# Weight requests regrouped and more blocks begun early around the first two token tiles of a linear-attention and snake-MLP kernel

## The chip, the cores and the metric

The kernel runs on one core of one Trainium2 chip. The metric is the device time of one execution in microseconds (us). The kernel before has a median of 282.01 us over three runs (281.81, 282.01 and 282.65).

The core has a matrix engine (TensorE, "PE" in the profile, its weight loads "PEld"), VectorE ("DVE"), ScalarE ("ACT"), GpSimd ("POOL") and SyncE ("SP"). SP and GpSimd issue the DMA transfers here. Each engine has its own instruction order, fixed when the kernel is built, and waits for the others through semaphores.

## What is computed

Two functions follow each other. The first is linear attention over 8 batches, 8 heads, 576 positions and a head size of 64; the second is a feed-forward block with a snake activation, from 512 to 2048 features and back:

```python
q_s = softmax(q, axis=-1)            # over the 64 features
k_s = softmax(k, axis=2)             # over the 576 positions
kv = np.einsum('bhsd,bhse->bhde', k_s, v)
attn_out = np.einsum('bhsd,bhde->bhse', q_s, kv)
x = attn_out.transpose(0, 2, 1, 3).reshape(4608, 512)
h = x @ w_in
s = np.sin(alpha * h)
g = h + s * s / (alpha + 1e-09)
out = g @ w_out
```

Inputs and output are float32; the kernel works in bfloat16 with float32 sums.

## The kernel before

**Tiling.** The 4608 tokens are worked on in nine tiles of 512 (`nT`). For a tile, the 2048 features of `h` are 16 blocks of 128 (`nN`). One block of `h` is four matmuls of 128x512 (`mm_h`, L275), one for each chunk of 128 features of `x`; the chunks are taken in the order 0, 2, 1, 3 (`KO`, L261). A call of `mm_h` may do a part of the four, so that a block is begun early and ended later. A block then goes through `sine` (L286: a sine on ScalarE, and a square on ScalarE, GpSimd or VectorE, as a letter A, P or D says) and `combine` (L297: VectorE, which writes the block of `g`). `h_slot` (L431) does these for one block, and `flush` lets the combine run one block behind. In tiles 0 and 1, `h_slot` takes the first 4 and 2 blocks as already begun with two of their chunks.

**PSUM banks.** Every block of `h` needs a bank. `BANKS` (L266) says which pool a block of a tile takes its bank from: a, b and l have two banks each, and k is one larger buffer. For tile 1 the string is "aakbbllaabbllaab": blocks 0 and 1 take the two a banks, block 2 the k buffer, 3 and 4 the b banks, 5 and 6 the l banks, 7 and 8 the a banks again, 9 and 10 the b banks again, and so on. A bank can be written again when the combine of the block that had it before is done.

**The second product.** `g @ w_out` is 4 row groups of 128 tokens by 16 blocks of w_out's rows, 64 matmuls for a tile (`mm_o`, L301). For tile 0 it runs through `o_quad` (L439), which keeps all four sums open in the banks of b, b, l and l and goes by quarters of the 16 row blocks: 0 to 3, 4 to 7, 8 to 11, 12 to 15. A sum that is complete is copied out of PSUM (`evac_o`) by the engine that is named for it. `o_quad` and `o_stream` (L591, the form for the later tiles) are generators: `take(os, n)` emits the next n matmuls at that place of the program, and `take(os)` all that are left. In `o_stream` for tile 1, the first two row groups do blocks 0 to 13 each and then 14 and 15 each.

**Attention in between.** The x of tile 0 comes from batch 0, and most of the x of tile 1 from batch 1. While tile 0's `o_quad` runs, batch 1's q and k are exponentiated on ScalarE (`exp_half`), v is cast to bfloat16 (`cast_v1`, L495) on ScalarE, GpSimd and VectorE, `wide_mm` forms the product of k and v for half of the heads (18 matmuls of 128x130), `wide_norm` scales it on VectorE, and `attn_x` forms x for that half of the heads (4 matmuls on quarters of the array). After `attn_x(1, 0)`, ScalarE copies chunk 0 of x and VectorE chunk 2 into `xT`; after `attn_x(1, 1)`, VectorE copies chunks 1 and 3.

**Loads.** The weights are cast to bfloat16 by the DMA and are requested by GpSimd (`load_win`, L107; `load_wout`, L110). Before tile 0, GpSimd requests w_in in pieces, the last of them being columns 1536 to 2047 (blocks 12 to 15), and then w_out's row blocks 0 to 7. The rest is requested from inside tile 0's loop through the table `late` (L476): at block 6 the first half of batch 1's q, at 8 w_out's row blocks 8 to 11, at 10 row blocks 12 and 13, and at 12 the second half of q and then k and v of batch 1 in five requests (`load_kv1`, L468). q, k and v go through SP's queue, w_in and w_out through GpSimd's. Row blocks 14 and 15 come as float32 through SP's queue after batch 1's v into two spare tiles (L488) and are cast into `wout` later, one by GpSimd and one by ScalarE (L544). After them on SP's queue come the last 64 positions of q for batches 0 and 1 (`q8`) and the three loads of batch 2.

Of the kernel before, what the change touches and what calls it, by code (L numbers as in the profile page):

```python
# [15 lines left out]
F32 = mybir.dt.float32  # L16
# [7 lines left out]
def kernel(  # L24
# [14 lines left out]
    nc = tc.nc  # L39
# [7 lines left out]
    nN = d_ff // 128  # L47
    MF = 512
# [12 lines left out]
    spool = ctx.enter_context(tc.tile_pool(name="spool", bufs=4))  # L61
# [45 lines left out]
    def load_win(c0, c1, cc=slice(0, 4)):  # L107
        nc.gpsimd.dma_start(out=win[:, cc, c0:c1], in_=win_v[:, cc, c0:c1])  # L108

    def load_wout(n0, n1):  # L110
        nc.gpsimd.dma_start(out=wout[:, n0:n1, :], in_=wout_v[:, n0:n1, :])
# [151 lines left out]
    G = {}  # L263

    HP = {}
    BANKS = {0: "aabbkllaabbkllaa", 1: "aakbbllaabbllaab", 2: "aabbopaabbopaabb"}  # L266

    def bank(kind):
# [6 lines left out]
    def mm_h(t, ni, k0=0, k1=4):  # L275

        if ni == 0 and k0 == 0:
            G[t] = gpool.tile([128, nN, MF], BF16, name="g")
        hp = HP[t, ni] if k0 else bank(BANKS.get(t, 3 * "aabb" + "abba")[ni])
        HP[t, ni] = hp  # L280
        for k in range(k0, k1):
            nc.tensor.matmul(hp, win[:, KO[k], ni * 128:(ni + 1) * 128],  # L282
                             xT[:, KO[k], t * MF % NX:t * MF % NX + MF], start=(k == 0), stop=(k == 3))
        return hp
# [75 lines left out]
    load_win(0, 512, slice(1, 4, 2))  # L360
    for c in range(2, 6):
        load_win(256 * c, 256 * c + 256)
    load_win(1536, 2048)
    for c in range(2):
        load_wout(4 * c, 4 * c + 4)

# [62 lines left out]
        mm_h(0, ni, ki, ki + 1)  # L429

    def h_slot(t, ni, sq, lag):  # L431
        hp = mm_h(t, ni, 2 if ni < (4, 2, 0)[min(t, 2)] else 0)
        lag.append((t, ni, hp, sine(t, ni, hp, sq)))

    def flush(lag, keep):
# [15 lines left out]
    def take(it, n=1000):  # L451
        for _ in range(n):
            if next(it, 0) == 0:
                return
# [4 lines left out]
    with ES:  # L459
        def load_q1(ii):  # L460
            if ii == 0:
                staged["q", 1] = stage.tile([128, 4, J, D], F32, name="st_q", tag="st")
            st = staged["q", 1]
            DVE_CP(st[:, ii, 0, 0:1], zero)
            nc.sync.dma_start(out=st[:, ii::2, 0:8].rearrange("p i j d -> p i (j d)"),
                              in_=src_view(q, 1)[:, ii::2, 0:8 * D])

        def load_kv1():  # L468
            for n in "kv":
                staged[n, 1] = stage.tile([128, 4, J, D], F32, name=f"st_{n}", tag="st")  # L470
            for n, t, ii, j0, j1 in (("k", k, 0, 0, J), ("v", v, 0, 0, J), ("k", k, 1, 0, J),
                                     ("v", v, 1, 0, 5), ("v", v, 1, 5, J)):
                nc.sync.dma_start(out=staged[n, 1][:, ii::2, j0:j1].rearrange("p i j d -> p i (j d)"),
                                  in_=src_view(t, 1)[:, ii::2, j0 * D:j1 * D])

        late = {6: lambda: load_q1(0), 8: lambda: load_wout(8, 12), 10: lambda: load_wout(12, 14),  # L476
                12: lambda: (load_q1(1), load_kv1())}
        for ni in range(nN):
            h_slot(0, ni, "DPPAPPAPPAAPPAPD"[ni], lag)
            flush(lag, 1)  # L480
            if ni in late:
                late[ni]()
        flush(lag, 0)

        accs = [bank(kind) for kind in "bbll"]
        os = o_quad(0, accs, [DVE_CP, ACT_CP, DVE_CP, DVE_CP])

        late_w = [spool.tile([128, MF], F32, name="s") for _ in range(2)]  # L488
        for n in range(2):
            nc.sync.dma_start(out=late_w[n], in_=wout_v[:, 14 + n])  # L490
        for b in range(2):
            nc.sync.dma_start(out=q8[:, :, b], in_=src_view(q, b)[:, :, 8 * D:J * D])
        load_batch(2)
# [34 lines left out]
        exp_half("k", 1, 1)  # L528
        take(os, 9)
        transpose_q1(1, DVE_CP)  # L530
        take(os, 1)
        wide_mm(1, 0)
        wide_norm(1, 0)
        take(os, 3)
        cast_v1(1)
        xa = [bank("a") for _ in range(2)]
        attn_x(1, 0, 0, 8, xa)
        for x in range(2):
            (ACT_CP, DVE_CP)[x](xT[:, 2 * x, MF:2 * MF], xa[x])
        take(os, 1)  # L540
        wide_mm(1, 1)
        wide_norm(1, 1)
        for n, eng in ((0, GP_CP), (1, ACT_CP)):
            eng(wout[:, 14 + n], late_w[n])  # L544
        exp_to(A["qe", 1][:, J - 2:J], q8)
        for ni, ki in ((0, 0), (1, 0), (0, 1), (1, 1)):
            mm_h(1, ni, ki, ki + 1)
        xb = ps_k.tile([128, 2, MF], F32, name="kvp", tag="a")
        attn_x(1, 1, 0, 8, [xb[:, x] for x in range(2)])
        DVE_CP(xT[:, 1:4:2, MF:2 * MF], xb)  # L550
        nc.scalar.activation(zero, zero, AX.Sin)
        take(os)
        scale_q8 = norm_q8()
        load("q", q, 3)
        load("k", k, 3)
# [35 lines left out]
    def o_stream(t, eng=DVE_CP):  # L591
        order = [(j, ni) for j in range(4) for ni in range(nN)]
        if t == 1:
            order = [(j, ni) for n0, n1 in ((0, nN - 2), (nN - 2, nN)) for j in range(2) for ni in range(n0, n1)] + order[2 * nN:]
        acc = {}
        for j, ni in order:
            if ni == 0:
                acc[j] = bank("b" if t == 1 and j == 0 else "op"[j % 2])
            mm_o(t, j, ni, acc[j])
            if ni == nN - 1:  # L600
                evac_o(t, j, acc[j], eng)
            yield
# [4 lines left out]
    os = o_stream(1)  # L607
# [131 lines left out]
```

## Time and profile before

| | |
|---|---|
| median of three runs | 282.01 us |
| the profiled execution | 283.14 us |
| its span, first to last instruction | 281.3 us |
| TensorE busy | 268.4 us, 95% of the span |
| ScalarE busy | 224.2 us, 80% |
| VectorE busy | 187.1 us, 67% |
| GpSimd busy | 80.2 us, 28% |
| granted TensorE clock | 0.999 of full speed |

The profile is of one execution. Its span leaves out what lies before the first and after the last instruction. Matmuls are pipelined: a 128x512 matmul is shown with some 379 ns, but the next one starts earlier, so the distance of starts is what tells how fast they run, and a busy TensorE need not be at its peak. A few matmul records are missing, so a group can show three where four were run. A line number can be that of a helper, as for `mm_h` (its matmul is L282) and `mm_o` (L302).

The time by stretches of the program shows where the edits lie (from the span's start; busy time of each engine in us):

| stretch, us | what TensorE does | PE | DVE | ACT | POOL | DMA, GB/s |
|---|---|---|---|---|---|---|
| 0 to 13 | batch 0's attention | 7.28 | 7.97 | 8.96 | 7.68 | 289 |
| 13 to 24.55 | tile 0, blocks to 11 | 10.75 | 7.92 | 10.23 | 8.23 | 187 |
| 24.55 to 35.39 | tile 0's last blocks, w_out rows 0 to 7 | 10.54 | 8.81 | 7.22 | 4.57 | 268 |
| 35.39 to 43.38 | w_out rows 8 on, batch 1's attention | 7.78 | 5.54 | 4.32 | 1.65 | 384 |
| 43.38 to 59.81 | tile 1's blocks | 16.32 | 14.86 | 15.20 | 8.78 | 323 |
| 59.81 to 75.60 | w_out for tile 1, batch 2's attention | 15.58 | 15.16 | 13.74 | 10.92 | 239 |
| 75.60 to 100 | tile 2 | 24.24 | 17.92 | 21.44 | 15.63 | 188 |
| 100 to 281.30 | tiles 3 to 8 | 175.96 | 108.96 | 143.13 | 22.70 | 113 |

### The profile page before, as it was taken

What the parts mean: (1) busy time and instruction counts of PE and PEld (TensorE: products, weight loads), DVE (VectorE), ACT (ScalarE), POOL (GpSimd) and SP (SyncE); (2) the same over time, 40 slices, a digit from 0 to 9 for tenths busy, and PEclk for the clock granted to TensorE, in tenths of its full rate; (3) what the DMA queues carried; (4) which work ended last, traced back from release to release, by engine and by line L of the source; (5) the groups of instructions that cost most, each with busy time, mean ns of one, the idle gap of its engine ahead of it and who ended that gap; (6) DMA issues with size and microseconds to landing.
All of it is one profiled execution on the core that took longest, in us unless ns stands there. A gap on an engine that the chain in (4) does not pass through costs nothing.

```text
span 281.3 us, 4775 instructions
## 1 busy us (share of the span) xinstructions
PE 268.4 (95%) x1814; PEld 124.2 (44%) x1843; DVE 187.1 (67%) x279; ACT 224.2 (80%) x321; POOL 80.2 (28%) x75
## 2 busy tenths in 40 slices
PE   3899999999999999999999999999999999999994
PEld 1434454444444444444444444444444444444443
DVE  2968867999878767766776677577775555555422
ACT  4799457999588999899989998999877777777400
POOL 2959112678667450215011500350000000000000
PEclk9999999999999999999999999999999999999999
DMA  7999999795699039811981199125011111111143
GB/s 258 299 185 224 276 385 401 266 356 198 156 245 379 3 76 294 336 37 43 328 332 37 40 267 384 37 51 123 10 30 37 37 40 37 38 42 44 41 100 75
DMA packets 39607, 46.06 MB, mean 164 GB/s; under 512 B 17040, under 2 KB 22944, under 8 KB 39584
## 3 DMA queue, kind: packets, MB, share of 16 engines
q1 hardware_dynamic: 33952, 41.11, 46.1%
q0 software_dynamic: 5472, 4.52, 9.8%
q8 instruction: 14, 0.23, 0.3%
q10 hardware_dynamic: 160, 0.13, 0.2%
q14 instruction: 9, 0.07, 0.1%
HBM read 36.71 MB, written 9.44 MB: 164 GB/s over the span
## 4 chain that ended last, share of the span: by engine, by line
PE 87%; DMA 8%; POOL 2%; issue 1%; ACT 0%; SPq 0%; DVE 0%
PE hp L282 38%; PE op L302 37%; DMA wout<-in_moe_w_out_dram 4%; PE hp L302 2%; DMA win<-in_moe_w_in_dram 2%; PE lp L282 2%; DMA st_k<-in_k_dram 2%; PE kvp L173 2%; PE lp L302 1%; PE op L282 1%; PE op L709 1%; PE hp L237 1%; POOL s L292 1%; PE xp L237 1%; PE kvp L282 1%
## 5 line engine op out<-in xcount | busy, mean ns | idle before, releaser
L298 DVE SCALAR_TENSOR_TENSOR g<-s,inva_sb,hp 128x512 bf16<-128x512 f32 x129 | 95.1, 745 | 58.9 <-ACT s L290 53.3
L282 PE MATMUL hp<-xT,win 128*128 128x512 bf16 x508 | 128.8, 379 | 0.8 <-DMA win<-in_moe_w_in_dram 0.4
L302 PE MATMUL op<-wout,g 128*128 128x512 bf16 x463 | 117.6, 379 | 1.7 <-issue 1.3
L288 ACT ACTIVATE s<-hp,alpha_sb 128x512 f32<-128x512 f32 x129 | 87.0, 684 | 21.8 <-PE hp L282 20.3
L282 PEld LDWEIGHTS <-win 128*128 128x128 bf16 x576 | 55.6, 98 | 68.4 <-DMA win<-in_moe_w_in_dram 1.8
L302 PEld LDWEIGHTS <-g 128*128 128x128 bf16 x560 | 53.4, 98 | 65.4 <-issue 2.9
L290 ACT ACTIVATE s<-s 128x512 f32<-128x512 f32 x112 | 70.7, 632 | 3.6
L292 POOL TENSOR_TENSOR s<-s 128x512 f32<-128x512 f32 x28 | 29.5, 1066 | 17.8 <-ACT s L288 17.7
L152 POOL TENSOR_TENSOR qn<-qe,qs 128x1152 bf16<-128x1152 bf16 x11 | 23.2, 2128 | 30.7 <-DVE qs L146 26.3
L314 DVE COPY o<-op 128x512 f32<-128x512 f32 (+2 forms) x32 | 21.1, 660 | 9.7 <-PE op L302 7.4
L137 POOL CAST vb<-st_v 128x1152 bf16<-128x1152 f32 x12 | 14.4, 1228 | 44.5 <-DMA st_v<-in_v_dram 44.2
L118 ACT ACTIVATE qe<-st_q 128x1152 bf16<-128x1152 f32 (+2 forms) x18 | 17.7, 1026 | 6.3 <-DMA st_q<-in_q_dram 6.1
L118 ACT ACTIVATE ke<-st_k 128x1152 bf16<-128x1152 f32 x16 | 17.9, 1153 | 2.6 <-DMA st_k<-in_k_dram 2.6
L145 DVE TENSOR_REDUCE qs<-qe 128x36 f32<-128x2304 bf16 x5 | 12.8, 2552 | 8.3 <-ACT qe L118 8.3
L302 PE MATMUL hp<-wout,g 128*128 128x512 bf16 x45 | 12.0, 379 | 0.5 <-DMA wout<-in_moe_w_out_dram 0.3
L118 ACT ACT_TABLE_LOAD x7 | 9.0, 1283 | 0.8 <-PEq L723 0.7
L302 PE MATMUL lp<-wout,g 128*128 128x512 bf16 x32 | 9.2, 379 | 0.1
L369 PE MATMUL warm<-st_q,ident 128*128 128x512 f32 (+1 forms) x6 | 4.1, 806 | 4.7 <-DMA st_q<-in_q_dram 4.7
L282 PE MATMUL lp<-xT,win 128*128 128x512 bf16 x32 | 7.7, 379 | 0.4 <-DMA win<-in_moe_w_in_dram 0.4
L250 DVE CAST xT<-xp 128x1024 bf16<-128x1024 f32 (+1 forms) x7 | 7.4, 1065 | 0.0
L298 DVE SCALAR_TENSOR_TENSOR g<-s,inva_sb,lp 128x512 bf16<-128x512 f32 x8 | 5.7, 739 | 0.4 <-POOL s L292 0.4
L108 POOL DMA_DIRECT2D win<-in_moe_w_in_dram x8 | 5.9, 772 | 0.0
(98 smaller groups left out, 137.2 us busy)
## 6 DMA issues: line engine op xcount, KB each, us to landing
out_dram<-o SPq DMA_DIRECT2D x70, 128.0 KB, 2.3
st_q<-in_q_dram SPq DMA_DIRECT2D x6, 1152.0 KB, 6.3
st_k<-in_k_dram SPq DMA_DIRECT2D x6, 1152.0 KB, 9.1
st_v<-in_v_dram SPq DMA_DIRECT2D x6, 1152.0 KB, 11.3
st_k<-in_k_dram SPq DMA_DIRECT2D x4, 576.0 KB, 8.3
st_q<-in_q_dram SPq DMA_DIRECT2D x4, 512.0 KB, 6.2
wout<-in_moe_w_out_dram POOLq DMA_DIRECT2D x3, 512.0 KB, 13.7
win<-in_moe_w_in_dram POOLq DMA_DIRECT2D x5, 256.0 KB, 7.9
```

The costliest lines, as they stand in the source:

```text
L118: nc.scalar.activation(dst[:, :, ii * 128:(ii + 1) * 128].rearrange("p j (x d) -> p x j d", x=2), src[:, ii::2], AX.Exp)
L137: engs[ii](vv[:, 2 * ii:2 * ii + 2, :, 0:D], staged["v", b][:, ii::2])
L145: nc.vector.tensor_reduce(qs, A["qe", b].rearrange("p j (i d) -> p j i d", i=4), axis=AXL.X, op=ALU.add)
L152: engs[ii % len(engs)].tensor_tensor(qn[:, ii, 0:j1].rearrange("p j (x d) -> p j x d", x=2), qe[:, ii], part.unsqueeze(3).to_broadcast([12 ...
L250: eng(xT[:, c, d0:d0 + m - n], xp[..., n:m])
L282: nc.tensor.matmul(hp, win[:, KO[k], ni * 128:(ni + 1) * 128], xT[:, KO[k], t * MF % NX:t * MF % NX + MF], start=(k == 0), stop=(k == 3))
L288: nc.scalar.activation(s, hp, AX.Sin, scale=alpha_sb[:, ni:ni + 1])
L290: nc.scalar.activation(s, s, AX.Square)
L292: nc.gpsimd.tensor_tensor(s, s, s, op=ALU.mult)
L298: nc.vector.scalar_tensor_tensor(G[t][:, ni], in0=s, scalar=inva_sb[:, ni:ni + 1], in1=hp, op0=ALU.mult, op1=ALU.add)
L302: nc.tensor.matmul(acc, G[t][:, ni, j * 128:(j + 1) * 128], wout[:, ni, :], start=(ni == 0), stop=(ni == nN - 1))
L314: eng(o[:, cols], acc)
```

## The change

Seven edits, all in the first two tiles:

1. The last w_in piece (columns 1536 to 2047) is requested in two parts, chunks 0 and 2 first, then 1 and 3.
2. w_out's row blocks 8 to 11 are requested in two parts, 8 and 9 at block 8 of tile 0's loop and 10 and 11 at block 10.
3. Row blocks 12 to 15 are requested by GpSimd in two parts at block 14. The float32 tiles for 14 and 15, their two requests on SP's queue and the two casts are gone. GpSimd's requests for 12 to 15 now stand behind three more squares in its order, those of blocks 11, 12 and 14.
4. In tile 0, blocks 12 and 13 both do chunks 0 and 2 before block 12 goes on.
5. Around batch 1's attention, more of `o_quad` is taken before each step (6 instead of 1 before the first `wide_mm`, 3 instead of 1 after the first `attn_x`), so that both wide products come later; one matmul is left for the last `take`. The sums are copied out by ScalarE, VectorE, ScalarE, VectorE.
6. In tile 1, blocks 0, 1, 3, 4 and 5 are begun early: 0, 1 and 3 with three of the four chunks, 4 and 5 with two (the table `BEGUN`). Chunks 1 and 3 of x are copied one by one by VectorE.
7. In `o_stream` for tile 1 the first pass ends at block 12 instead of 14.

TensorE runs the same 1840 matmuls; their order changes between the end of tile 0's blocks and tile 1's w_out.

```diff
+    BEGUN = {0: {ni: 2 for ni in (0, 1, 2, 3, 12, 13)}, 1: {0: 3, 1: 3, 3: 3, 4: 2, 5: 2}}
...
-    load_win(1536, 2048)
+    for r in range(2):
+        load_win(1536, 2048, slice(r, 4, 2))
...
-        hp = mm_h(t, ni, 2 if ni < (4, 2, 0)[min(t, 2)] else 0)
+        hp = mm_h(t, ni, BEGUN.get(t, {}).get(ni, 0))
...
-        late = {6: lambda: load_q1(0), 8: lambda: load_wout(8, 12), 10: lambda: load_wout(12, 14),
-                12: lambda: (load_q1(1), load_kv1())}
+        late = {6: lambda: load_q1(0), 8: lambda: load_wout(8, 10), 10: lambda: load_wout(10, 12),
+                12: lambda: (load_q1(1), load_kv1()), 14: lambda: (load_wout(12, 14), load_wout(14, 16))}
         for ni in range(nN):
+            for n in (12, 13) if ni == 12 else ():
+                mm_h(0, n, 0, 2)
...
-        os = o_quad(0, accs, [DVE_CP, ACT_CP, DVE_CP, DVE_CP])
-
-        late_w = [spool.tile([128, MF], F32, name="s") for _ in range(2)]
-        for n in range(2):
-            nc.sync.dma_start(out=late_w[n], in_=wout_v[:, 14 + n])
+        os = o_quad(0, accs, [ACT_CP, DVE_CP, ACT_CP, DVE_CP])
+
...
         transpose_q1(1, DVE_CP)
-        take(os, 1)
+        take(os, 6)
         wide_mm(1, 0)
         wide_norm(1, 0)
         take(os, 3)
-        cast_v1(1)
         xa = [bank("a") for _ in range(2)]
         attn_x(1, 0, 0, 8, xa)
         for x in range(2):
             (ACT_CP, DVE_CP)[x](xT[:, 2 * x, MF:2 * MF], xa[x])
-        take(os, 1)
+        cast_v1(1)
+        take(os, 3)
+        for ni, ki in ((0, 0), (1, 0), (0, 1), (1, 1)):
+            mm_h(1, ni, ki, ki + 1)
         wide_mm(1, 1)
         wide_norm(1, 1)
-        for n, eng in ((0, GP_CP), (1, ACT_CP)):
-            eng(wout[:, 14 + n], late_w[n])
         exp_to(A["qe", 1][:, J - 2:J], q8)
-        for ni, ki in ((0, 0), (1, 0), (0, 1), (1, 1)):
+        take(os)
+        for ni, ki in ((3, 0), (3, 1), (4, 0)):
             mm_h(1, ni, ki, ki + 1)
         xb = ps_k.tile([128, 2, MF], F32, name="kvp", tag="a")
         attn_x(1, 1, 0, 8, [xb[:, x] for x in range(2)])
-        DVE_CP(xT[:, 1:4:2, MF:2 * MF], xb)
+        for x in range(2):
+            DVE_CP(xT[:, 2 * x + 1, MF:2 * MF], xb[:, x])
         nc.scalar.activation(zero, zero, AX.Sin)
-        take(os)
+        for ni, ki in ((4, 1), (5, 0), (5, 1), (0, 2), (1, 2), (3, 2)):
+            mm_h(1, ni, ki, ki + 1)
...
-            order = [(j, ni) for n0, n1 in ((0, nN - 2), (nN - 2, nN)) for j in range(2) for ni in range(n0, n1)] + order[2 * nN:]
+            order = [(j, ni) for n0, n1 in ((0, 12), (12, nN)) for j in range(2) for ni in range(n0, n1)] + order[2 * nN:]
```

## Prediction

> **What bounds the kernel now.** I read the page's busy times and chain first, then TensorE's waits, then the time-ordered rows of each engine from 13 to 75 us, where every edit lies.
>
> ```profile
> PE 268.4 (95%) x1814; PEld 124.2 (44%) x1843; DVE 187.1 (67%) x279; ACT 224.2 (80%) x321; POOL 80.2 (28%) x75
> ...
> PE 87%; DMA 8%; POOL 2%; issue 1%; ACT 0%; SPq 0%; DVE 0%
> ```
>
> TensorE is the bound: the chain that ends last runs through it for 87% of the span, and the DMA share is the places where it stood waiting for a load. The edits keep TensorE's work the same, so they can only move its waits. TensorE's waits from 13 to 80 us, and its rows around two of them (start, duration, operation, count, idle time before and what ended it):
>
> ```profile
> PE lp L282 <- DMA win<-in_moe_w_in_dram: 0.4, 1, 0.4
> PE hp L282 <- DMA win<-in_moe_w_in_dram: 0.4, 1, 0.4
> PE hp L302 <- DMA wout<-in_moe_w_out_dram: 0.3, 1, 0.3
> ...
> 23.36 0.81 PE L282 MATMUL kvp<-xT,win 128*128 128x512 bf16 x3
> 24.55 1.90 PE L282 MATMUL lp<-xT,win 128*128 128x512 bf16 x8 [0.39 <-DMA win<-in_moe_w_in_dram]
> ...
> 34.49 0.59 PE L302 MATMUL lp<-wout,g 128*128 128x512 bf16 x2
> 35.39 0.38 PE L302 MATMUL hp<-wout,g 128*128 128x512 bf16 x1 [0.30 <-DMA wout<-in_moe_w_out_dram]
> ```
>
> Back to back, eight 128x512 matmuls start over 1.73 us (24.55 to 26.29), 0.216 us each; the 379 ns of the groups overlap. So starts give the true stalls. Block 11 (kvp, four matmuls, one record missing) should hand over at 23.36 + 4 x 0.216 = 24.22, and block 12 begins at 24.55: 0.33 us lost to the last w_in piece. The pair at 34.49 should hand over at 34.92, and row block 8 begins at 35.39: 0.47 us lost to w_out. The third wait (15.57) lies before every edit.
>
> **Part 1, two requests for the last w_in piece and for w_out 8 to 11: -0.80 us.** The first half of w_in serves chunks 0 and 2, and now blocks 12 and 13 both do these first: the second half is wanted 4 x 0.216 us after 24.22, at 25.08, and the whole piece was there by 24.55. Rows 8 and 9 are wanted at 34.92 - 0.33 = 34.59. The four rows took 35.35 - 31.07 = 4.3 us of their queue (landings of the last two w_out requests, issue plus time to landing), so half of them land near 33.2. Rows 10 and 11 are wanted 8 x 0.216 later, at 36.3, and land near 35.35. Both stalls go, 0.80 us. GpSimd issues one more request before the first square (0.75 us); it sits idle 2.48 us there. The bounds are -0.80 and, if neither half lands early, 0.
>
> The Trainium skill, "DMA: Bandwidth & Descriptors", Rules for kernel authors, advises at least 1 MiB per transfer for full bandwidth, which speaks against halves. Here the four w_in requests of 256 KB written before the last land 1.28 to 1.34 us apart, and the 512 KB one 3.31 us after them, so halves are not slower in this trace; if they were, 0.33 us of the gain would be in doubt.
>
> **Part 2, w_out 12 to 15 on GpSimd's queue: +0.9 us, with part of it from k.** Rows 12, 13 (256 KB as written) were requested at 25.34 right behind 8 to 11. Now they come after square 14, at about 29.3, and 14, 15 after them at 30.1. They ran on SP's queue behind v before, into a float32 tile, with a cast each on GpSimd (0.61) and ScalarE (0.62), both casts with idle time before them; taking these away gives TensorE nothing. SP's queue loses those two requests, so batch 2's loads (first issued at 39.46) go out sooner, but behind v in the same queue, and cost k and v nothing. Two queues share the DMA engines there, and what each gets is seen in the DMA view for 32 to 33 us and in the stretches (the last two figures are DMA share and GB/s):
>
> ```profile
> q1 hardware_dynamic: 95, 0.19, 56.9%
> q0 software_dynamic: 92, 0.09, 54.1%
> ...
> 35.00:37.00 2.00, 1.64 (x8) 0.78 (x8) 0.92 (x1) 1.05 (x1) 0.00 (x0) 1.00 1.05 397
> 37.00:39.00 2.00, 2.00 (x17) 1.13 (x15) 1.93 (x4) 1.17 (x1) 0.00 (x0) 1.00 1.04 400
> 39.00:41.00 2.00, 2.00 (x27) 1.19 (x26) 0.87 (x2) 0.88 (x2) 0.62 (x1) 1.00 1.08 392
> ```
>
> q0 is GpSimd's queue, q1 is SP's: packet for packet they alternate, and a q0 packet of half the bytes costs the engines as much. From 35 to 41 us the engines are full with k and v of batch 1. Alone, q0 moves 209 GB/s (30 to 31 us), so 256 KB more of it takes 262 KB / 209 GB/s = 1.25 us of all engines, and k and v behind it land up to that much later. Bounds: 0 (all of it after k) and 1.45 (16 packets for each DMA engine at 0.09, half of the 0.18 us between shared ones).
>
> What waits for k is on ScalarE:
>
> ```profile
> 40.85 1.17 ACT L118 ACTIVATE ke<-st_k 128x1152 bf16<-128x1152 f32 x1 [0.70 <-DMA st_k<-in_k_dram]
> 42.56 0.59 ACT L539 CAST xT<-hp 128x512 bf16<-128x512 f32 x1 [0.54 <-PE hp L237]
> ...
> 47.58 0.69 ACT L288 ACTIVATE s<-hp,alpha_sb 128x512 f32<-128x512 f32 x1
> ```
>
> The second half of k is exponentiated the moment it lands, and x's chunk 0 is copied behind it. The change puts a PSUM evacuation (0.57) between them. With k at 40.85 + 1.25 = 42.10: exponential to 43.15 (1.05 where two follow each other), evacuation to 43.65, copy to 44.24, seen by TensorE at 44.28. TensorE wants that chunk for block 0 of tile 1. Before, it got there at 43.38; now 0.80 earlier by part 1, seven w_out matmuls later (63 against 56 done; 1.51), without the second wide product (0.62 and 0.1 for the change of tile shape): 43.38 - 0.80 + 1.51 - 0.72 = 43.37. The wait is 44.28 - 43.37 = 0.91. With k on time the copy ends at 43.03, 0.34 ahead: 0 is the lower bound, and 1.45 gives 1.1.
>
> Rows 14, 15 lie inside this. They are wanted at 40.38 - 0.80 + 5 x 0.216 = 40.66. Rows 12, 13 landed 2.94 us after 8 to 11 while sharing, so the like piece behind lands at 38.29 + 2.9 = 41.2 (stall 0.55); at the lone rate 39.5 (none). A stall there only spends part of the 0.91, because k is waited for in any case. GpSimd's and VectorE's casts of v have more room: the second wide product comes 0.9 us after the chunk.
>
> **Part 3, three matmuls instead of eight ahead of chunk 1: +0.15.** attn_x of the second half starts at T; its copy started 0.46 later (44.35, 44.81), and half of it takes 0.69, ready at T + 1.15. TensorE: 0.34 + 3 x 0.216 = T + 0.99. Bounds 0 and 0.3.
>
> **Part 4, blocks begun early: +0.94.** This is the largest new wait. Blocks 0, 1 and 3 have three of four chunks before the first sine can run, 4 and 5 two. From the start of block 0's last matmul, at t, TensorE has 1 + 1 + 4 + 1 + 2 + 2 + 3 x 4 = 23 matmuls to block 9, which it reaches at t + 4.97; before, 31 (6.7). Block 9 takes the bank of block 3, free when VectorE has combined block 3:
>
> ```profile
> 49.43 1.41 DVE L298 SCALAR_TENSOR_TENSOR g<-s,inva_sb,hp 128x512 bf16<-128x512 f32 x2 [0.77 <-POOL s L292]
> 50.75 1.00 DVE L294 TENSOR_TENSOR s<-s 128x512 f32<-128x512 f32 x1
> 51.68 0.73 DVE L298 SCALAR_TENSOR_TENSOR g<-s,inva_sb,kvp 128x512 bf16<-128x512 f32 x1
> 52.33 1.39 DVE L298 SCALAR_TENSOR_TENSOR g<-s,inva_sb,hp 128x512 bf16<-128x512 f32 x2
> ```
>
> First sine 47.58, GpSimd's square to 49.39, then VectorE without a gap until block 3 is combined at 52.33 + 0.74 = 53.07: 5.49 us that the change doesn't shorten. A sine starts 0.42 after its block's last matmul (76.21 to 76.63 in tile 2). The bank is free at t + 5.91; the wait is 5.91 - 4.97 = 0.94. Bounds: 0.63 if the square at 50.75 takes the 0.69 of the one at 29.60, 1.1 if ScalarE adds a wait.
>
> The Trainium skill, "Advanced Engine Details and Errata", VectorE Performance Modes, says that GpSimd shares VectorE's second SBUF port, so the two block each other. The slow square lies beside GpSimd's 50.17 to 52.66; by that rule it stays 1.00 as long as the two stay neighbours, which they do, so I keep 0.94.
>
> After block 9 ScalarE paces the tile and the delay is passed on; TensorE has no slack later to take it back. The two blocks fewer in o_stream's first pass cost nothing: block 12 is wanted 5.2 us after it starts, and the last combine followed it by 3.3.
>
> **Sum:** -0.80 + 0.91 + 0.15 + 0.94 = +1.20. The profiled span becomes 281.3 + 1.2 = 282.5. The profiled execution took 283.14 with its span of 281.3, and the runs shown have a median of 282.01; I put the same difference on it: 283.2 us.
>
> **Rivals.**
> - *k is not late* (the rows fill gaps or come behind k): -0.80 + 0.15 + 0.94 = +0.3, 282.3. For it: the bounds of part 2. Against: no free DMA time in the stretches.
> - *Faster: TensorE loses only its waits.* If block 3's combine ends 0.9 us sooner after the first sine, because squares and evacuations no longer crowd VectorE (it had 0.77 idle ahead of 49.43), and k is on time, -0.80 remains: 281.2; decides if the wait at block 9 is under 0.1. Against: the chain is GpSimd's square plus five VectorE operations in a row.
> - *The loads slip further:* GpSimd's late requests give rows 12, 13 after 38.49, when they are wanted (landing 38.29, 0.2 to spare), and k a further 1 us: 0.91 + 1.0 in part 2, 284.2. For it: the small margin.
> - *The edits don't act* (the halves land together): part 1 gives 0 and all else stands, 284.0; counted with the last.
>
> **How the numbers follow.** A measurement of this kernel tells 0.3% (0.85 us) from no change: 281.16 to 282.86. Chances: forecast 0.48 (own range 282.7 to 283.6; 0.06 of it under the bound), k on time 0.24, only waits lost 0.14 (0.10 of it past the bound), slipping loads or no action 0.14. Faster 0.10, same 0.34, slower 0.56. The range reaches from the second rival, 281.3, to the third, 284.2.
>
> **What would show it.** Right: no wait at the lp of block 12 nor at row 8; a ScalarE exponential of k starting near 42.1 and TensorE waiting for ScalarE's copy of xT before block 0 of tile 1; a TensorE wait for VectorE of 0.6 to 1.1 us at block 9 of tile 1. Wrong: k's exponential at or before 41.2, or block 9 begun without a wait; then the time is 0.9 lower for each.

## The result: 284.04 us, 0.6% slower

| | before | changed |
|---|---|---|
| median, six runs each | 282.39 us (281.81 to 282.80) | 284.04 us (283.92 to 284.24) |
| first profiled execution | 283.14 us, span 281.3 us | 284.09 us, span 282.3 us |
| second profiled execution | 281.94 us, span 280.1 us | 283.74 us, span 282.0 us |

The changed kernel takes 1.0061 of the time before, 95% interval 1.0047 to 1.0074; a second measurement (below) gives 1.0053, 1.0034 to 1.0072. It is slower, as forecast, and inside the range of 281.3 to 284.2. It is 0.84 us above the forecast of 283.2, though, and above the forecast's own range of 282.7 to 283.6. Part of the 0.84 is the base: the prediction had three runs of the kernel before (282.01), and the median of six is 282.39. As a difference, +1.20 was forecast and +1.65 measured (+1.48 the second time). The forecast's parts were not all right, and the second execution of the kernel before, read below, is what tells them apart.

First the page of the changed kernel, first execution: the busy line, and the chain that ended last by engine.

```profile
PE 272.3 (96%) x1843; PEld 125.3 (44%) x1843; DVE 187.0 (66%) x279; ACT 223.8 (79%) x321; POOL 81.9 (29%) x77
...
PE 82%; DMA 5%; issue 4%; DVE 3%; ACT 3%; POOL 2%; SPq 0%; POOLq 0%; ACTq 0%
```

The 3.9 us more of busy TensorE are no work: this trace has all matmul records (1843 for 1843 weight loads; before, 1814). What is new is in the chain: VectorE and ScalarE now hold 3% of it each (GpSimd had its 2% before, too), and the loads 5% instead of 8%. TensorE's waits from 13 to 80 us show where (line, releaser: us in total, times, longest):

```profile
PE hp L283 <- DVE g L299: 0.9, 1, 0.9
```

The two waits for w_in and the one for w_out that this view showed before are gone, and one wait for a combine has come. Its place is in the time-ordered rows of TensorE (start, duration, operation, count, and in brackets the idle time before and what ended it):

```profile
51.41 1.89 PE L283 MATMUL hp<-xT,win 128*128 128x512 bf16 x8
54.18 1.02 PE L283 MATMUL hp<-xT,win 128*128 128x512 bf16 x4 [0.89 <-DVE g L299]
```

The eight matmuls are blocks 7 and 8 of tile 1; at 0.216 us a start they should hand over at 51.41 + 1.73 = 53.14, and block 9 starts at 54.18: 1.05 us lost (the 0.89 counts from the drawn end of the last matmul). VectorE's rows of the same execution:

```profile
50.49 1.41 DVE L299 SCALAR_TENSOR_TENSOR g<-s,inva_sb,hp 128x512 bf16<-128x512 f32 x2 [1.59 <-POOL s L293]
51.81 1.00 DVE L295 TENSOR_TENSOR s<-s 128x512 f32<-128x512 f32 x1
52.74 0.73 DVE L299 SCALAR_TENSOR_TENSOR g<-s,inva_sb,kvp 128x512 bf16<-128x512 f32 x1
53.39 1.39 DVE L299 SCALAR_TENSOR_TENSOR g<-s,inva_sb,hp 128x512 bf16<-128x512 f32 x2
```

Block 3 is the first of the pair at 53.39 and is done by 54.13; TensorE goes on 0.05 later. It is the same row of five operations behind GpSimd's square as before, 1.06 us later. What ScalarE does ahead of it:

```profile
41.15 1.16 ACT L118 ACTIVATE ke<-st_k 128x1152 bf16<-128x1152 f32 x1 [1.24 <-DMA st_k<-in_k_dram]
...
43.04 0.59 ACT L539 CAST xT<-hp 128x512 bf16<-128x512 f32 x1 [0.23 <-PE hp L237]
...
48.64 1.27 ACT L289 ACTIVATE s<-hp,alpha_sb 128x512 f32<-128x512 f32 x2 [2.23 <-PE hp L283]
```

k's second exponential starts at 41.15, only 0.30 later than in the first profile of before (40.85), and the copy of chunk 0 waits for TensorE rather than TensorE for it. By this comparison k would hardly be late. That comparison misleads, as the first experiment shows.

### The profile page after: what moved, and what is told of

Its sections match the earlier page's. It is cut to its first block, busy times and chain, and to the rows that moved or that the text cites. A ratio compares the mean times of both kernels' runs of the same rounds, so it can differ in the third digit from the quotient of the medians.

```text
span 282.3 us, 4801 instructions
## 1 busy us (share of the span) xinstructions
PE 272.3 (96%) x1843; PEld 125.3 (44%) x1843; DVE 187.0 (66%) x279; ACT 223.8 (79%) x321; POOL 81.9 (29%) x77
## 4 chain that ended last, share of the span: by engine, by line
PE 82%; DMA 5%; issue 4%; DVE 3%; ACT 3%; POOL 2%; SPq 0%; POOLq 0%; ACTq 0%
PE op L303 37%; PE hp L283 35%; DMA st_v<-in_v_dram 3%; ACT s L289 2%; PE warm L371 2%; PE kvp L173 2%; DVE g L299 2%; POOL s L293 1%; DMA st_q<-in_q_dram 1%; PE op L283 1%; PE hp L303 1%; PE op L713 1%; PE hp L237 1%; PE xp L237 1%; PE lp L283 1%
## 5 line engine op out<-in xcount | busy, mean ns | idle before, releaser
L303 PE MATMUL op<-wout,g 128*128 128x512 bf16 x480 | 120.4, 379 | 0.0
L303 PE MATMUL hp<-wout,g 128*128 128x512 bf16 x48 | 12.8, 379 | 0.0
L371 PE MATMUL warm<-st_q,ident 128*128 128x512 f32 (+1 forms) x6 | 4.9, 958 | 4.7 <-DMA st_q<-in_q_dram 4.7
L108 POOL DMA_DIRECT2D win<-in_moe_w_in_dram x9 | 6.6, 783 | 0.0
```

Source lines behind the costliest of these rows:

```text
L303: nc.tensor.matmul(acc, G[t][:, ni, j * 128:(j + 1) * 128], wout[:, ni, :], start=(ni == 0), stop=(ni == nN - 1))
L371: nc.tensor.matmul(warm.rearrange("p a b -> p (a b)")[:, 0:n], ident, staged["q", 0][:, 0, 0:8].rearrange("p j d -> p (j d)")[:, 0:n], sta ...
```

## The experiments

Twelve runs followed, in groups of four, four, two and two, with the kernel before measured again beside each group (medians 282.29, 282.06, 281.93 and 282.08 us over 15 to 21 runs); the ratios are to those. "Lost" is by how much the distance between two matmul starts exceeds the one at the same place in before_again or, where the order is new, the one between such matmuls when nothing is waited for. Where a matmul's record is missing (its weight load is there), its own 0.216 us are taken off. Losses under 0.1 are left out, and so is the start of tile 0, which comes 0.8 us later in fewer_begun, 0.5 in win_split_only and 0.1 in late_rows than in before_again.

| run | median, us | ratio, 95% interval | span of its profile | what TensorE lost between 13 and 62 us |
|---|---|---|---|---|
| before_again | 282.39 | 1.0009 [0.9988, 1.0030] | 280.1 | nothing |
| after_again | 283.77 | 1.0053 [1.0034, 1.0072] | 282.0 | 1.05 block 9; 0.24 w_out row 14; 0.37 copy of chunk 0; 0.21 chunk 1 |
| dma_only | 283.87 | 1.0054 [1.0036, 1.0072] | 281.4 | 0.96 and 0.20 at casts of v |
| begin_only | 285.33 | 1.0102 [1.0074, 1.0131] | 284.2 | 1.05 block 9; 0.21 chunk 1; 0.19 copies of chunks 0 and 2; 1.76 and 0.41 w_out; 0.78 w_in |
| k_at_9 | 285.48 | 1.0111 [1.0093, 1.0128] | 283.1 | 0.39 block 9; 1.69 and 0.27 q's transposes; 0.32 cast of v; 0.38 copy of chunk 0; 0.21 chunk 1 |
| fewer_begun | 284.24 | 1.0061 [1.0041, 1.0080] | 283.1 | none at block 9; 0.87 and 0.38 chunk 1; 0.48 cast of v; 0.40 copy of chunk 0 |
| split_only | 282.47 | 1.0014 [1.0001, 1.0027] | 280.4 | 0.54 at a combine of tile 0 |
| rows_at_10 | 284.78 | 1.0092 [1.0076, 1.0109] | 283.0 | 1.26 at a combine of tile 0; 1.05 block 9; 0.21 chunk 1; 0.19 copies of chunks 0 and 2; 0.14 q's second transposes |
| late_rows | 283.41 | 1.0046 [1.0030, 1.0063] | 281.8 | 1.05 block 9; 0.21 chunk 1; 0.19 copies of chunks 0 and 2 |
| win_split_only | 282.48 | 1.0008 [0.9993, 1.0022] | 281.3 | 0.71 w_out row 8; 0.10 w_in's second half |
| three_three | 281.92 | 0.9996 [0.9986, 1.0007] | 280.0 | nothing |
| before_third | one run, 281.95 | | 280.1 | nothing |

### before_again and after_again: the same two kernels, profiled a second time

> The kernel before, once more, with a profile of its own. Theory 'order' (the waits at w_in's last piece and at w_out row 8 belong to the kernel and come in every execution): stalls of about 0.33 and 0.47 us again, span 281 to 281.6, ratio 1.000. Theory 'chance' (the first profile caught loads that are late only now and then, which would explain why the medians differ by 1.65 us and the two profiles' TensorE rows by 0.83): one of the stalls is missing here and the span is 0.4 to 0.8 us shorter.

> The changed kernel, once more. Theory 'order': a wait of 0.9 to 1.1 us at block 9 of tile 1 again, 0.2 before chunk 1, none at w_in or w_out; ratio 1.005 to 1.007. If the slow first transposes (8.21 to 9.27 us) of its first profile were chance, its tile 0 starts 0.5 us earlier here and the span is near 281.8; if they belong to the kernel, they are there again.

TensorE's waits from 13 to 80 us, kernel before, second execution, all that the view lists:

```profile
PE hp L302 <- issue: 0.2, 1, 0.2
PE op L302 <- issue: 0.2, 1, 0.2
```

No wait for a load is left; the two lines of 0.2 are missing matmul records. The chain on this execution's page says the same in one line, against the 87% and 8% of the first:

```profile
PE 96%; DMA 1%; issue 1%; DVE 0%
```

So the three load waits of the first profile do not come in every execution. Whether row 8 of w_out is waited for goes by when the request for rows 8 to 11 lands. The list of DMA issues from 24 to 45 us (count, size, median us from issue to landing), kernel before, first execution:

```profile
wout<-in_moe_w_out_dram POOLq DMA_DIRECT2D x1, 512.0 KB, 10.8
```

and the second:

```profile
wout<-in_moe_w_out_dram POOLq DMA_DIRECT2D x1, 512.0 KB, 8.9
```

1.9 us between two executions of one program, where the stall was 0.47. The first one had been measured at 283.14 us when the median of its runs was 282.01: it was one of the longer executions, and the 0.80 us of stalls are of the size of that difference.

The same goes for k. ScalarE's rows in the second execution of before:

```profile
39.55 1.16 ACT L118 ACTIVATE ke<-st_k 128x1152 bf16<-128x1152 f32 x1 [0.69 <-DMA st_k<-in_k_dram]
...
46.43 1.27 ACT L288 ACTIVATE s<-hp,alpha_sb 128x512 f32<-128x512 f32 x2
```

and in the second execution of the changed kernel:

```profile
41.27 1.16 ACT L118 ACTIVATE ke<-st_k 128x1152 bf16<-128x1152 f32 x1 [0.92 <-DMA st_k<-in_k_dram]
...
48.31 1.26 ACT L289 ACTIVATE s<-hp,alpha_sb 128x512 f32<-128x512 f32 x2 [1.88 <-PE hp L283]
```

Compared like with like, k's exponential comes 1.72 us later, not 0.30, and the first sine of tile 1 1.88 us later. The waits of the changed kernel in this execution:

```profile
PE hp L283 <- DVE g L299: 0.9, 1, 0.9
PE hp L283 <- ACT xT L539: 0.2, 1, 0.2
```

Now TensorE does wait for ScalarE's copy of chunk 0, as the prediction had it (0.37 by starts), after 0.24 for w_out's row 14, the 57th matmul of the sum, which starts at 40.36 as its load lands, too short a stop for this view. In the first execution of the changed kernel TensorE began tile 0 at 13.57 us instead of 12.68, which gave k 0.9 us more: its lateness was hidden by another one. With 0.21 at chunk 1, the changed kernel loses 1.05 + 0.24 + 0.37 + 0.21 = 1.87 us by these places; its span is 282.0 - 280.1 = 1.9 us longer.

### dma_only: the loads' edits with tile 1 as before

```diff
 against the changed kernel
-        os = o_quad(0, accs, [ACT_CP, DVE_CP, ACT_CP, DVE_CP])
+        os = o_quad(0, accs, [DVE_CP, ACT_CP, DVE_CP, DVE_CP])
...
-        take(os, 6)
+        take(os, 1)
         wide_mm(1, 0)
...
```

The rest of edits 5 to 7 is taken back in the same way; edits 1 to 4 stay.

> Edits 1 to 4 alone: the requests and tile 0's order; batch 1's attention and tile 1 as before. Theory 'order' (the loss is tile 1's order, the gain the requests): no wait at block 9, both stalls gone, TensorE 0.6 to 0.8 us earlier from row 8 on, unless k is late; ratio 0.997. Rival 'requests' (the loss comes from w_out's rows sharing the DMA engines with k and v): k's second exponential starts 0.5 us or more later and TensorE waits for x's chunk 0 of tile 1; ratio 1.002 or more.

TensorE's waits, 13 to 80 us:

```profile
PE kvp L184 <- ACT vb L499: 0.9, 1, 0.9
```

The loads' edits alone cost as much as the whole change. In the old order TensorE reaches the first wide product of batch 1 at 39.3 and loses 0.96 us to ScalarE's cast of v, and 0.20 more before the second. No wait at block 9. The late loads are a loss of 1.2 us in this execution (1.3 by the spans; 1.6 by the medians, the profiled execution being the quickest of nine) when nothing is put in front of them; the changed order of tile 1 puts five more w_out matmuls there, and in after_again the waits for casts of v are gone.

Why k and v are late is seen in one microsecond, 36 to 37 us, in the queues of the kernel before, second execution (packets, MB, share of 16 DMA engines):

```profile
q1 hardware_dynamic: 189, 0.41, 104.6%
```

and of the changed kernel, second execution:

```profile
q1 hardware_dynamic: 98, 0.21, 59.5%
q0 software_dynamic: 102, 0.09, 53.6%
```

SP's queue (q1), which carries k and v, moves half of what it moved, and the two queues alternate packet by packet: 98 to 102. The Trainium skill, "DMA: Bandwidth & Descriptors", section "Queues, rings and completion order", says that each DMA engine goes round between the queues it has work for, a packet at a time; these counts agree. Since a packet of GpSimd's queue carries less here (0.09 MB in 102 against 0.21 in 98), the DMA engines moved 0.30 MB in this microsecond where they had moved 0.41.

### begin_only: the new order of tile 1 with the old loads

```diff
 against the changed kernel
-    for r in range(2):
-        load_win(1536, 2048, slice(r, 4, 2))
+    load_win(1536, 2048)
...
+        late = {6: lambda: load_q1(0), 8: lambda: load_wout(8, 12), 10: lambda: load_wout(12, 16),
+                12: lambda: (load_q1(1), load_kv1())}
...
-            for n in (12, 13) if ni == 12 else ():
-                mm_h(0, n, 0, 2)
```

> Edits 5 to 7 with the requests of before (w_out 8 to 11 in one request; 12 to 15 in one request at block 10, since the new order wants 14 and 15 earlier than the float32 tiles have them). Theory 'order': the wait of about 1 us at block 9 is here too, and the two stalls of before: ratio 1.003 to 1.008. Rival 'requests': no wait at block 9 beyond 0.3 us, ratio 1.000 or less.

TensorE's waits, 13 to 80 us:

```profile
PE hp L303 <- DMA wout<-in_moe_w_out_dram: 1.8, 2, 1.6
PE hp L283 <- DVE g L299: 0.9, 1, 0.9
PE lp L283 <- DMA win<-in_moe_w_in_dram: 0.6, 1, 0.6
```

Four rows in one request came too late for row 12 (1.76 us), a stall that neither kernel has, so its time says little. What it does show: the wait at block 9 is 1.05 again when w_out's rows are requested another way. k is not early here (its second exponential starts at 41.90), so late_rows repeats the question without these rows.

### late_rows: the new order with k and v alone on the DMA engines

```diff
 against the changed kernel
-        nc.tensor.matmul(acc, G[t][:, ni, j * 128:(j + 1) * 128], wout[:, ni, :],
+        nc.tensor.matmul(acc, G[t][:, ni, j * 128:(j + 1) * 128], wout[:, ni - 4 * (t == 0 and ni > 11), :],
...
-                12: lambda: (load_q1(1), load_kv1()), 14: lambda: (load_wout(12, 14), load_wout(14, 16))}
+                12: lambda: (load_q1(1), load_kv1())}
...
         cast_v1(1)
+        load_wout(12, 16)
```

Tile 0's sums leave rows 12 to 15 out and read rows 8 to 11 again, in as many matmuls.

> The changed kernel without the late loads' traffic: rows 12 to 15 of w_out are requested behind the second cast of v, some 12 us later, and tile 0's output reads rows 8 to 11 a second time in their place (that tile's values are so changed; all later tiles read the right rows). k and v then share the window with nothing. Theory 'order': the new order of tile 1 costs its 1.05 at block 9 and 0.2 at chunk 1 whatever the loads do; the excesses of 0.24 at 39.9 and 0.37 at 42.9 vanish, v lands 1.5 us earlier or more, and the median is 1.2 to 1.4 above the kernel before, 283.2 to 283.5, ratio 1.004 to 1.005. Rival 'requests': block 9's wait is only the lateness of k and v handed on; with early loads it falls below 0.4 and the median is within 0.5 of the kernel before. Rival 'GpSimd': the one later request holds GpSimd for some 1 us in front of its cast or square, the wait at chunk 1 or at block 9 grows, and the median is at 283.8 or above.

TensorE's waits, 13 to 80 us, all but two of 0.2 that are missing records:

```profile
PE hp L283 <- DVE g L299: 0.9, 1, 0.9
```

Its rows at the start of tile 1:

```profile
42.39 0.82 PE L303 MATMUL lp<-wout,g 128*128 128x512 bf16 x3
43.14 1.13 PE L283 MATMUL hp<-xT,win 128*128 128x512 bf16 x4
```

The theory "order" holds: the wait for row 14 is gone, block 9's is 1.05 to the hundredth, and the median is 1.48 us above the kernel before (283.41 against 281.93). k's second exponential starts at 38.30, far from mattering, and yet 0.19 is lost at block 0: three matmuls from 42.39 hand over at 43.04 and the next starts at 43.14, when ScalarE's copy of chunk 0 (42.50 to 43.09) is done, and a matmul later TensorE stops 0.10 for VectorE's copy of chunk 2, whose bank block 1 takes. By starts the new order loses 1.05 + 0.21 + 0.19 = 1.45. The 0.19 does not hang on k, and no step of the prediction had it. The order alone (1.48) and the loads alone (1.58, dma_only) each cost about what the whole change costs (1.48, after_again): they do not add up.

### fewer_begun: seven early matmuls instead of thirteen

```diff
 against the changed kernel
-... 1: {0: 3, 1: 3, 3: 3, 4: 2, 5: 2}}
+... 1: {0: 2, 1: 2, 3: 2, 4: 1}}
...
-        for ni, ki in ((4, 1), (5, 0), (5, 1), (0, 2), (1, 2), (3, 2)):
-            mm_h(1, ni, ki, ki + 1)
```

> The changed kernel without the six matmuls of blocks 0, 1, 3, 4 and 5 between the first sine's table load and the block loop: they go back to their blocks, the other seven early ones stay. Theory 'first sine': these six cover the two copies of chunk 1; without them TensorE waits 1.0 to 1.3 us for the copies, the first sine starts at the same time or up to 0.3 earlier, and block 9 is reached after block 3's combine, so the wait of 1.05 there vanishes; what is saved at one place is lost at the other and the median stays within 0.3 of 283.8, ratio 1.004 to 1.006. Rival 'early starts cost': the six push block 0's last matmul and so the first sine back by their own 1.3 us, and without them the sine starts 1 us earlier and the median falls by 0.7 or more, to about 283.0.

TensorE's rows:

```profile
48.28 0.38 PE L283 MATMUL hp<-xT,win 128*128 128x512 bf16 x1 [0.80 <-DVE xT L553]
48.88 0.81 PE L283 MATMUL hp<-xT,win 128*128 128x512 bf16 x3 [0.22 <-DVE xT L553]
...
53.19 3.19 PE L283 MATMUL hp<-xT,win 128*128 128x512 bf16 x14
```

The stall moves from block 9 to the copies of chunk 1, and blocks 7 to 10 run through without one (the view ends at 56 us and shows 14 of their 16 matmuls). At the copies 0.87 + 0.38 = 1.25 us are lost, where after_again loses 0.21 there and 1.05 at block 9, 1.26 together. The median of 284.24 is 0.47 above after_again's, more than the 0.3 of the expectation, with intervals that overlap; the rival (283.0) is out. So these six early matmuls neither gain nor lose: TensorE waits for the tile's first sines either ahead of them or behind them.

### k_at_9: another bank for block 9

```diff
 against the changed kernel
-    BANKS = {... 1: "aakbbllaabbllaab", ...}
+    BANKS = {... 1: "aakbbllaakbbllaa", ...}
...
-            if ni == 11:
+            if ni == 13:
                 tp = ps_k.tile([128, 2, 2, 128], BF16, name="tp", tag="a")
```

> The changed kernel with one more turn of the k bank in tile 1: block 9 accumulates there (it waits for block 2's combine instead of block 3's), blocks 10 to 15 each go one bank on, and the late transposes of q move from block 11 to block 13. Theory 'bank': the wait at block 9 is set by the combine that frees its bank; block 2's combine ends 0.66 us before block 3's (52.40 to 53.06 begin, 0.7 each), so the wait of 1.05 us falls to about 0.4, block 10 waits no more than 0.1, and the median falls by 0.65 to 283.1 to 283.4, ratio to the kernel before 1.002 to 1.004. Rival 'the sine chain sets the end': VectorE and ScalarE finish the tile no sooner whatever bank is used, so TensorE loses the 0.65 again at a later block of tile 1 or at the first rows of tile 1's output, and the median stays at 283.8 to 284.0. Rival 'k bank': the late transposes now wait for block 9's combine, 0.5 or more, and nothing is gained.

TensorE's rows:

```profile
53.08 1.02 PE L283 MATMUL kvp<-xT,win 128*128 128x512 bf16 x4 [0.23 <-DVE g L299]
...
59.08 0.38 PE L567 MATMUL tp<-identb,qe 128*128 128x128 bf16 x4 [1.52 <-ACT s L291]
```

VectorE's row for block 9:

```profile
58.29 0.73 DVE L299 SCALAR_TENSOR_TENSOR g<-s,inva_sb,kvp 128x512 bf16<-128x512 f32 x1
```

Half of the theory is shown: block 9 waits for the combine that frees its bank, and a bank freed one combine earlier takes 0.66 off the wait (1.05 to 0.39). The other half is the rival "k bank" ("0.5 or more"), at 1.69: the transposes of q need that same bank, block 9 leaves it at 58.29 + 0.73 = 59.0, and TensorE starts them at 59.08. (The view names a ScalarE square that ends at 59.05; by the program the transposes need no square, but the bank.) The other bank moved the stall and made it larger.

### split_only, rows_at_10, win_split_only: what a request on GpSimd costs

split_only is the kernel before with part 1 alone, rows 8 to 11 both requested at block 8:

```diff
 against the kernel before
+    for r in range(2):
+        load_win(1536, 2048, slice(r, 4, 2))
...
+        late = {6: lambda: load_q1(0), 8: lambda: (load_wout(8, 10), load_wout(10, 12)), 10: lambda: load_wout(12, 14),
...
+            for n in (12, 13) if ni == 12 else ():
+                mm_h(0, n, 0, 2)
```

> The kernel before with the parts that can take a load's stall away and nothing else: the last piece of w_in in two requests, blocks 12 and 13 of tile 0 begun with their first two k, and rows 8 to 11 of w_out in two requests, both at block 8. Rows 12 to 15, k, v and tile 1 as in the kernel before. Theory 'the stalls were chance': no wait at block 12 or row 8 here, and the median equals the kernel before within 0.3 us (282.1 to 282.6, ratio 0.999 to 1.001), since most of its executions do not have these stalls either. Rival 'the stalls are usual': the median falls by 0.5 to 0.8 to 281.6 to 281.9, ratio 0.997 to 0.998.

It gains nothing and is 0.4 us slower, at the edge of what can be told. Its only new wait is 0.54 us for a combine at 28.6. rows_at_10 shows that wait enlarged:

```diff
 against the changed kernel
+                10: lambda: (load_wout(10, 12), load_wout(12, 14), load_wout(14, 16)),
+                12: lambda: (load_q1(1), load_kv1())}
```

> The changed kernel with rows 12 to 15 of w_out requested at block 10, right behind rows 10 and 11, and so 2.5 us ahead of the requests for k and v rather than among them. Theory 'gap': the 1 to 2 us in which GpSimd's queue moves nothing (about 32 to 34 us, SyncE's queue alone at 380 to 409 GB/s) disappear, rows 14 and 15 land at 38 to 39 instead of 40.3, k's and v's last pieces land 0.3 to 0.8 earlier than 41.2 and 42.8, the excesses of 0.24 and 0.37 at 39.9 and 42.9 vanish, and the median falls by 0.3 to 0.6. Rival 'bytes ahead': both queues together move the same bytes, k's first piece and q's second half land up to 1 us later, k's second exponential follows, and the median rises by 0.3 to 1. Rival 'no matter': block 9's wait absorbs it, within 0.2 of 283.8.

GpSimd's rows:

```profile
24.16 2.92 POOL L111 DMA_DIRECT2D wout<-in_moe_w_out_dram  x4
27.07 3.06 POOL L293 TENSOR_TENSOR s<-s 128x512 f32<-128x512 f32 x3
```

and TensorE's:

```profile
29.98 1.24 PE L303 MATMUL lp<-wout,g 128*128 128x512 bf16 x5 [1.09 <-DVE g L299]
```

Four requests hold GpSimd for 2.92 us, 0.73 each, and three squares stand behind them; a combine comes late, and TensorE loses 1.26 us. That was neither the theory nor a rival of mine. Rows 14 and 15 did land at 38.8, and the waits of 0.24 and 0.37 are gone, but TensorE came 1.26 later, which covers them by itself; k's and v's last pieces landed 0.3 later than in after_again, not earlier, so "gap" is wrong. The Trainium skill, "DMA: Bandwidth & Descriptors", section "SWDGE vs HWDGE vs iDMA", says that for a request from GpSimd its cores compute the descriptors in software; the 0.73 us of GpSimd's time agrees.

win_split_only leaves w_out's requests alone:

```diff
 against the kernel before
-    load_win(1536, 2048)
+    for r in range(2):
+        load_win(1536, 2048, slice(r, 4, 2))
```

> The kernel before with the last piece of w_in in two requests and nothing else. Theory 'GpSimd's time': in the run with rows 8 to 11 in two requests the third request of 0.73 us on GpSimd pushed a square of tile 0 back and TensorE waited 0.54 at 28.6 us; with as many requests in the block loop as the kernel before this wait is gone, and the median equals the kernel before within 0.3 (ratio 0.999 to 1.001). Rival 'the split itself': a fifth request of w_in ahead of w_out's rows costs 0.2 to 0.5 by the start of tile 0, ratio 1.001 to 1.002 without any wait at 28.6.

TensorE's waits, 13 to 80 us:

```profile
PE hp L302 <- DMA wout<-in_moe_w_out_dram: 0.5, 1, 0.5
```

The wait at 28.6 is gone, as "GpSimd's time" says. But now row 8 stalls by 0.71 in the profiled execution, which at 283.13 us is the slowest of its twelve, and tile 0 begins 0.5 later than in before_again. The rival "the split itself" had named such a start, but split_only and three_three split the piece in the same way and begin tile 0 on time (12.76 and 12.70 against 12.81). The median is 0.55 above the before beside it, outside the expected 0.3, but the interval of the ratio holds 1, so split and no split are not told apart.

### three_three and before_third: can the stalls be taken away for a gain?

```diff
 against split_only
-        late = {6: lambda: load_q1(0), 8: lambda: (load_wout(8, 10), load_wout(10, 12)), 10: lambda: load_wout(12, 14),
+        late = {6: lambda: load_q1(0), 8: lambda: load_wout(8, 11), 10: lambda: load_wout(11, 14),
```

> The kernel before with w_in's last piece in two requests, blocks 12 and 13 of tile 0 begun with two k, and rows 8 to 13 of w_out in two requests of three rows instead of four and two: as many requests on GpSimd as in the kernel before, but row 8 lands earlier. k, v, rows 14 and 15 and tile 1 as before. Theory 'stalls are worth something': neither load is waited for and no square is pushed back, so the median is 0.1 to 0.4 below the kernel before, ratio 0.9985 to 0.9995. Rival 'chance': most executions of the kernel before have nothing to win, the median is the same within 0.1 us and only the slowest executions differ. Rival 'row 11': the second request of three rows lands behind 37.1 us, when row 11 is wanted, and the median is 0.2 or more above.

> The kernel before, a third profile. If the stalls at w_in's last piece and at row 8 come and go by execution, they follow the landing of w_out's rows 8 to 11: with a landing at 33 us (as in the second profile) no stall at row 8 and a span near 280.1, with a landing behind 35 us (as in the first) 0.4 to 0.7 us of stall and a span of 280.8 to 281.3.

Rows 8 to 10 land at 31.5, nothing waits, no square is pushed back, and the median is 281.92 against 282.08: the same. before_third has no stall either; its request for rows 8 to 11 took 8.9 us and its span is 280.1, as expected of a landing at 33. Over all profiles, row 8 stalled in 3 of 5 with rows 8 to 11 in one request and in none of 9 with a smaller first one; the last w_in piece stalled in 2 of 4 and, in halves, by no more than 0.1 us in 10. The smaller requests do remove the stalls. But the median hardly falls: by the interval of its ratio (0.9986 to 1.0007) three_three gains at most 0.4 us, and perhaps nothing, where the first profile of the kernel before showed 0.80. No version here is faster than the kernel before by more than can be told.

## Why the prediction was right in its answer, and where its steps were not

**Part 4, block 9's wait (0.94): right.** It came at block 9, for block 3's combine, at 1.05 us, in each profile with the new order and the old banks and all thirteen early matmuls. The bank was forecast free 5.91 us after the start of block 0's last matmul; it took from 48.17 to 54.18, 6.01, since the first sine starts 0.48 behind that matmul where I had 0.42. VectorE's slow square stayed at 1.00, as assumed. late_rows and begin_only show that the loads have no part in the wait, and k_at_9 that the bank does. "TensorE has no slack later to take it back" held: the changed kernel is longer by what it lost here.

**Part 3, chunk 1 (0.15): right, 0.21.**

**Part 2, k and v behind w_out's rows (0.91): the mechanism right, the sizes off.** Packets alternate as read, and k is late by 1.72 us against a like execution, where I had 1.25. But I counted from a k that was 1.3 us late already (40.85 in the first profile, 39.55 in the second), so the exponential was put at 42.10 and came at 41.27, and TensorE lost 0.61 at row 14 and chunk 0 instead of 0.91, row 14's 0.24 among it as "a stall there only spends part of the 0.91" said. The first execution, whose tile 0 began late, lost 0.19 in all at chunks 0 and 2, no more than late_rows without any w_out rows in the way. The line I had set for "wrong", k at or before 41.2 and then 0.9 less time, was met by the first execution (41.15), and the time was not lower: that line used the same late start. The 0.61 lies within the bounds of 0 and 1.1, but 0 was too low: the prediction let the copy of chunk 0 end 0.34 ahead with k on time, and late_rows loses 0.19 there. In the old order the same loads cost 1.2 (dma_only).

**Part 1, no more stalls (-0.80): the step that failed.** The working was right for the profiled execution, and the halves do what it says. The failure is in the last step of the sum: I took 0.80 off a profile of 283.14 us and put the result on a median of 282.01, as if the median contained those stalls. Two of the three profiles of the kernel before do not (281.94 and 281.95 us), and three_three, which removes them and leaves tile 1 as it was, gains at most 0.4. Without that term the sum is 0.91 + 0.15 + 0.94 = 2.00, where the places add up to 1.87 and the medians differ by 1.48 to 1.65. It is the price of the rival "the edits don't act", 284.0, for another reason: they act, on something that two of three profiles do not have. The measured 284.04 so fell to a branch with a chance of 0.14 (shared with "the loads slip further"), and that it comes so near is partly luck: with the six-run base of 282.39 the same sum gives 284.4. That the range held the result owes to its upper end, set by a rival that did not happen. "GpSimd issues one more request ... it sits idle there" was too light as well: split_only lost 0.54 to such a request. In the changed kernel this wait does not occur.

**The rivals.** "k is not late" is out by dma_only and late_rows. "TensorE loses only its waits" is out: block 9's wait never fell under 0.1 with the new order unless another took its place. "The loads slip further" is out: rows 12 and 13 landed at 36.8 and 37.5 in the two executions, before 38.49, and k no further than told above. The cheap casts and the shorter first pass of `o_stream` cost nothing, as said.

**What stays open.** The waits add up to 1.87 us and the spans differ by 1.9, while the medians differ by 1.5 to 1.65. The second profile of before (281.94) lies 0.35 to 0.45 below the medians of its group (282.29 and 282.39), that of the changed kernel (283.74) at its own (283.77), so an ordinary execution of before has some delay that this profile lacks; whether it is a part of the load stalls is not shown. Some executions of each kernel are 0.5 to 1 us longer than others, and I have profiles of three of before and two of the changed kernel only, so how much of k's lateness an average execution pays is not settled either: late_rows (1.0046) and after_again (1.0053) are not told apart. Why the DMA engines fed one execution's w_out 1.9 us later than another's was not tried.

## What to carry to other kernels

Before a stall is counted as a gain, hold the profiled execution against the median: if it is slower by about the size of the stall, the stall may be its own, and a second profile costs less than the wrong term. Work begun early on TensorE moved a wait here and did not remove it (1.25 us in one place, 1.26 in two), because the chain behind the first result (sine, square, combine, bank) kept its length; the bank that came free last said where the wait appeared. A request moved to GpSimd's queue has two prices: the engine's own time ahead of what stands behind it (0.73 us here), and every packet it puts between the packets of another queue.

## What I had not expected of the hardware

- Two executions of one program differed by 1.9 us in the landing of one 512 KB request (8.9 and 10.8 us after its issue), and by 1.3 us in k, without any change of its code.
- The start of tile 0 moved too: TensorE's first matmul of it came between 12.6 and 13.6 us over the profiles. In the first execution of the changed kernel 0.43 us of that was a wait for a cast of batch 0's v.
- Two queues together moved less than one alone: 0.30 MB in the microsecond from 36 to 37 us against 0.41, with all 16 DMA engines busy in both.
